# Attention and two feed-forward layers on one core: other PSUM banks for the first feed-forward, thresholds on ScalarE, mixed score tiles in four quadrants, other first and last transfers

## The chip, the core and the metric

The kernel runs on one core of a Trainium2 chip. The metric is the device time of one execution in microseconds (us), the median of the runs shown. Engines are named as in the profile: PE is the matrix engine (PEld its weight loads), DVE VectorE, ACT ScalarE, POOL GpSimd, SP the engine that issues nearly all transfers (DMAs). Each engine works through its own list of instructions in the order in which they stand there; semaphores hold an instruction until what it needs is done.

## What is computed

```python
def _attn_ref(q, k, v, tau):          # 4 batches, 8 heads, 576 tokens, head size 64
    scores = scale * np.matmul(q, k.transpose(0, 1, 3, 2))
    thresh = np.max(scores, axis=-1, keepdims=True) - tau
    scores = np.where(scores >= thresh, scores, -1000000000.0)
    scores = scores - np.max(scores, axis=-1, keepdims=True)
    attn = np.exp(scores)
    attn = attn / (np.sum(attn, axis=-1, keepdims=True) + 1e-09)
    return np.matmul(attn, v)

def _moe_ref(x, w_in, w_out, g_ln):   # 2304 tokens, 512 -> 1024 -> 512
    h = x @ w_in
    e = np.exp(h - np.max(h, axis=-1, keepdims=True))
    solu = h * (e / (np.sum(e, axis=-1, keepdims=True) + 1e-09))
    mu = np.mean(solu, axis=-1, keepdims=True)
    var = np.mean((solu - mu) ** 2, axis=-1, keepdims=True)
    return ((solu - mu) / np.sqrt(var + 1e-06) * g_ln) @ w_out

def _moe2_ref(x, w_in, w_out):        # 2304 tokens, 512 -> 2048 -> 512
    h = x @ w_in
    g = h * np.tanh(np.where(h > 20.0, h, np.log1p(np.exp(np.minimum(h, 20.0)))))
    return g @ w_out
```

Attention's output is regrouped to 2304 rows of 512, goes through the first feed-forward (`_moe_ref`) and then through the second (`_moe2_ref`).

## The kernel before

The 32 heads are worked off in 16 pairs. A pair has 576 query rows for each head: four full tiles of 128 rows for each head, and one mixed tile that holds the last 64 rows of both heads, so 9 score tiles a pair and 144 in all. For a score tile PE makes the scores in PSUM (lines 751 and 759), DVE takes the row maximum with a minus sign (line 765), ACT takes the exponential with that as its bias (line 766), POOL makes the threshold out of the same maximum, a 128x1 operation (line 768), and DVE masks the exponential by comparing score and threshold, and sums it (line 769). PE then turns the result with transposes (lines 796 to 801), ACT copies it out of PSUM (line 777), and PE multiplies it by v (line 846).

The first 8 pairs (`p < R0`) take their scores as plain float32 with the head's 64 channels split over two row halves of the array (`early`, line 751: one half makes the first 256 columns of keys, the other the last 320). A mixed tile does this twice there, once for each head, both adding into the same 128 output rows; the query columns of the other head are zeros. The last 8 pairs use split float32r products (`go`, line 759), for which ACT and POOL first make high and low parts of q and k (lines 717 to 723), with q scaled on POOL (line 721).

The first feed-forward runs on 18 tiles of 128 tokens: x times w_in (line 903), the softmax-times-h and the norm on DVE, ACT and POOL (lines 919 to 933), a transpose (line 952) and the product with w_out (line 973). Its products and transposes use two PSUM banks, `p_mo` 0 and 1, through `b_two`. Work of this stage stands between attention's score tiles, and goes on after the last of them.

The second feed-forward (line 1070) has 2016 products of 384 columns, in eight banks: six named `hoa`, which open when attention's own PSUM tiles are closed (`o_a`), and two named `hob`, which open when the first feed-forward is done (`o_c`). Its weights pass through rings of buffers `A7` and `B7`, loaded by SP; results gather in `acc` (line 1194) and leave by line 1218.

The order of all this is not written out by hand. `Plan` holds a task for each step with an engine, a duration and what it needs; `KEYS` gives each task a rank of three characters; `forward` walks through the tasks and takes for each engine the ready one with the best rank, with its own durations, rates and costs of changing PE's tile mode (`CHANGE`, by the `mode` of a task). The instructions are then written in that order, once, when the program is built. So any change of `KEYS`, of a duration or of a bank's rules gives another order on all engines.

At the start PE runs 11 products on zeros (`WARM`, line 549) while the first operands come in; ACT issues the load of tau, SP issues all others. Five small DVE operations make the scale and `nt8`, which holds minus tau, from tau (lines 552 to 556).

Of the kernel before, what the change touches and what calls it, by code (L numbers as in the profile page):

```python
# [19 lines left out]
    "io3bPeVUwaR9hdbeQVcd1hnVXPUdbHiNem8zcYDa4yca/gXgczbegzfFuaSHgQ3Y+8d3Fdl8bYnqPtfD0fHfZhWd7Rd51f+9icwYSEhLPfg2dxjb4rfZ0e+3"  # L20
    "f0Necsby5dbydYBdV1dr8aeSfWweFYfDYgpEfOjeujdbUdD9YCEdv6ibpcr4goDewob2sfaveAhb7nd6ZdjjbKlfc7Y1JdLYbvhayLa5PcwFbUpaXnfSWebq"
    "fiFaDNg7pdpGceUfQqcHYdIidYad5DcnAdeOdInaCHbjEdzTgn7cRfbYrbtceUXc7NdzLc21c5ZbuKchAfArdmxgCRc8vdLcbM+eNucswcnabINcgvZnUbJ+"
    "dwJdmWdtQboPdMcdjhdnjcRucpWccjemhbf6cAdc7YeAAcdudGbb3/eycbU8cUxbdQeJPegLa5Ad7IaWIbH1bNVciUbDIcaMbmnfxqZ2Md9kbOXW5RbYUX/1"
    "ZXPVoHYgnZflX3Dgh1cHCY8Ka2QdOsdAVY/pXSFaNrY/wbblY+aWP1ZckYhrdSpXlzVlHZ4OaoaYqeZP2ZNDX0YX4ObdYXdcZZdai/YQTYnaZMBXlpaOAbe1"
    "aaMa4QY1yYpfZqaYnCZ66WtFacBaYnbCqafKZzmYsUbCNaZLYd1YP6bDOWfiXlGbKTXwYXvnW+DXjWXS7bb2ZDCcZxZ7/WytZ7eaOEYeBadzXg8XdpXzNYRF"
    "ZuYYimXEiV3BW7IXfRZVRX+UZj+YHxXn9ZTZW7CXGPZacYyIaYHY2hZiJa5NYFKXxKXtOY1BY74ZCaY0eXOCYNWZHPXQ3X1UXjqW1qZDcXifZKSXcxUaUYYu"
    "Wt3ZcCajPXTjTdDYLEZRPa9QYEiaGvXAsZqOWaqVnMXe6YwIWhOYspYdxXjpZU+ZioYfPW3dYWbcryZLXX1MWVUb1/UjgVZJVs8ZgtWmyXS6UF5XbAZMyWW4"
    "ZNZVhOWsCW38VOcdLwWRuVaea8sXsPXM1U6NYuaWl7XWeWByV+YXhXW8IWSeUrGZO6aDYWgpX5CWx/VIsVk6V/xWi1WtPW37Uh0XBJV82b5qXoMYRiVejVN7"
    "VVzUoFWXRVuIZr+UlJXoPV2qV/hZ+KUheX4tRQvUW/UGjVoiWCHT9JaGNVrySzpXOeVsZU4yU5LYnpXCibbWZceVy4SivU1JVZhVdqWfiVAMUEeTx3Wt2TVN"
    "VVEXbeTrEXL8U//WrxUhLUsCU99WjkZSITiXWqRToEXf6UIlSphTScVeSX9iVpOTWWR5sTMtXdLYJAVaoSlDUCDUskUDOZtqXPpWCYVzrUT1WJhS+uTQ0SPn"  # L30
    "V73VbuVPiTtuYvgS8FSkLTXST9jTtLVnXVFhTzTRSLTrIUVFT8tR3qSbnVVJVGpUOkWbfTnUSeQT1TTunSCZUqmU2YU2XVjEVutTWKTZYT2NT81UpyS1ATZ1"
# [1254 lines left out]
```

## Time and profile before

| | us |
|---|---|
| median of 3 runs | 870.92 (869.85 to 874.6) |
| profiled execution | 871.98 |
| its span, first to last instruction | 870.2 |
| PE busy | 845.0 of 870.2, 97% |
| DVE busy | 738.5, 85% |
| ACT busy | 614.9, 71% |
| POOL busy | 294.1, 34% |
| TensorE clock granted | 1.00 throughout |

The busy share of an engine is an average over stages that are limited by different things. PE's busy time overlaps itself: a product's record is longer than the distance to the next one's start, so what PE really takes for a piece of work is read from one start to the next start.

### The profile page before, as it was taken

What the parts mean: (1) busy time and instruction counts of PE and PEld (TensorE: products, weight loads), DVE (VectorE), ACT (ScalarE), POOL (GpSimd) and SP (SyncE); (2) the same over time, 40 slices, a digit from 0 to 9 for tenths busy, and PEclk for the clock granted to TensorE, in tenths of its full rate; (3) what the DMA queues carried; (4) which work ended last, traced back from release to release, by engine and by line L of the source; (5) the groups of instructions that cost most, each with busy time, mean ns of one, the idle gap of its engine ahead of it and who ended that gap; (6) DMA issues with size and microseconds to landing.
All of it is one profiled execution on the core that took longest, in us unless ns stands there. A gap on an engine that the chain in (4) does not pass through costs nothing.

```text
span 870.2 us, 16492 instructions
## 1 busy us (share of the span) xinstructions
PE 845.0 (97%) x5423; PEld 736.9 (85%) x5423; DVE 738.5 (85%) x1638; ACT 614.9 (71%) x1292; POOL 294.1 (34%) x370
## 2 busy tenths in 40 slices
PE   7899999999999999999999999999999999999998
PEld 4556667878877888888789898999999999999998
DVE  6978888788788888899757897898999998968786
ACT  5898988877889878877545776856757664654551
POOL 2566665634756564532322211001121220000000
PEclk9999999999999999999999999999999999999999
DMA  7566444327745458445997689999999999888641
GB/s 238 177 210 191 141 149 127 116 77 244 207 138 151 126 158 267 132 133 151 299 391 237 193 252 325 343 306 363 305 336 302 305 298 348 279 276 275 198 136 72
DMA packets 155573, 195.22 MB, mean 224 GB/s; under 512 B 15312, under 2 KB 112608, under 8 KB 155488
## 3 DMA queue, kind: packets, MB, share of 16 engines
q1 hardware_dynamic: 155344, 194.17, 69.5%
q8 instruction: 43, 0.70, 0.3%
q14 instruction: 42, 0.34, 0.1%
q10 hardware_dynamic: 144, 0.00, 0.0%
HBM read 142.94 MB, written 51.19 MB: 223 GB/s over the span
## 4 chain that ended last, share of the span: by engine, by line
PE 83%; DVE 5%; DMA 4%; ACT 4%; issue 2%; POOL 2%; SPq 0%; POOLq 0%; ACTq 0%; DVEq 0%
PE hoa L1070 28%; PE p_mo L903 11%; PE hob L1070 9%; PE p_ta L846 9%; PE p_mo L973 9%; PE p_ta L796 6%; PE st L759 5%; PE st L751 4%; DMA B<-w2c 2%; PE p_mo L952 1%; DVE m L765 1%; DVE e L769 1%; PE p_ta L799 1%; ACT e L766 1%; DMA A<-w2c 1%
## 5 line engine op out<-in xcount | busy, mean ns | idle before, releaser
L1070 PE MATMUL hoa<-y,A 128*128 128x384 f32 x678 | 132.3, 336 | 1.8 <-ACT gf L1120 0.9
L769 DVE SCALAR_TENSOR_TENSOR e<-st,m,e 128x576 f32<-128x576 f32 x139 | 111.5, 814 | 18.0 <-POOL m L768 8.6
L765 DVE TENSOR_REDUCE m<-st 128x1 f32<-128x576 f32 x139 | 102.5, 753 | 24.6 <-PE st L751 12.4
L1070 PEld LDWEIGHTS hoa<-y,A 128*128 128x128 f32 x678 | 118.1, 188 | 3.1 <-ACT gf L1120 1.5
L766 ACT ACTIVATE e<-st,m 128x576 f32<-128x576 f32 x139 | 101.4, 741 | 23.6 <-DVE m L765 22.7
L1130 POOL TENSOR_TENSOR gf<-gf 128x384 f32<-128x384 f32 x24 | 24.4, 1017 | 232.4 <-DVE gf L1130 108.8
L1156 ACT ACTIVATE gh<-gf 128x384 fp32r<-128x384 f32 x168 | 80.4, 517 | 31.8 <-DVE gf L1130 11.5
L1070 PE MATMUL hoa<-gh,B 128*128 128x384 f32 x464 | 99.4, 335 | 0.6 <-DVE acc L1194 0.6
L1158 DVE TENSOR_TENSOR gl<-gf,gh 128x384 fp32r<-128x384 f32 x168 | 88.3, 563 | 1.5 <-PE hob L1070 1.2
L796 PE MATMUL p_ta<-ident,e 128*128 128x128 f32 x576 | 84.3, 276 | 3.7 <-ACT ex L777 1.3
L973 PE MATMUL p_mo<-LH,W2H 128*128 128x256 f32 x288 | 84.3, 293 | 1.2 <-DVE LL L958 1.2
L796 PEld LDWEIGHTS p_ta<-ident,e 128*128 128x128 f32 x576 | 65.6, 140 | 22.0 <-issue 3.6
L1070 PEld LDWEIGHTS hoa<-gh,B 128*128 128x128 f32 x464 | 82.0, 188 | 1.3 <-DVE acc L1194 1.1
L973 PE MATMUL p_mo<-LL,W2H 128*128 128x256 f32 x288 | 81.5, 283 | 0.1
L973 PE MATMUL p_mo<-LH,W2L 128*128 128x256 f32 x288 | 81.3, 282 | 0.0
L768 POOL TENSOR_SCALAR m<-m,cs 128x1 f32<-128x1 f32 x144 | 39.2, 275 | 119.8 <-DVE m L765 37.5
L612 POOL TENSOR_TENSOR ws<-cf,cl 128x512 uint32<-128x512 uint32 x32 | 41.3, 1289 | 103.5 <-DVE gl L1158 16.4
L1126 ACT ACTIVATE gf<-gf 128x384 f32<-128x384 f32 x72 | 37.2, 523 | 41.5 <-DVE gf L1123 41.2
L1194 DVE TENSOR_TENSOR acc<-acc,hoa 128x384 f32<-128x384 f32 x104 | 56.1, 550 | 8.0 <-PE hoa L1070 6.4
L903 PE MATMUL p_mo<-W1H,XH 128*128 128x512 f32 x144 | 60.8, 422 | 0.5 <-ACT ys L987 0.5
L1070 PE MATMUL hoa<-gl,B 128*128 128x384 f32 x232 | 59.2, 335 | 0.0
L973 PEld LDWEIGHTS p_mo<-LH,W2H 128*128 128x128 f32 x288 | 54.9, 191 | 3.9 <-issue 2.2
(127 smaller groups left out, 2171.0 us busy)
## 6 DMA issues: line engine op xcount, KB each, us to landing
...
```

Of the source, the lines that this page charges most:

```text
L759: TE.matmul(flat()[:, c0 + c:c0 + c + w], q.tile[:, i * 128:(i + 1) * 128], ks.tile[:, k0:k0 + w], start=(y == z == 0), stop=(y == len(hea ...
L765: t = add("DVE", dve(S), lambda: V.tensor_reduce(m.tile[:, 2:3], x(), AX.XY, ALU.max, negate=True), [t], [m], [st])
L766: a = add("ACT", act(S, True) + 0.1, lambda: SC.activation(et(), x(), ACTF.Exp, bias=m.tile[:, 2:3]), [t], [e] if h == 0 else (), [st, m, ...
L769: t = add("DVE", dve(S) + 0.06, lambda: V.scalar_tensor_tensor(et(), x(), m.tile[:, 1:2], et(), ALU.is_ge, ALU.mult, accum_out=sr.tile[:, ...
L796: TE.transpose(tp.tile[:, k * 128:(k + 1) * 128], e.tile[:, o:o + 128], ident)
L846: TE.matmul(acc.tile[h * 64:h * 64 + 64, :w], v.tile[:, k, h], r, start=(k == 0), stop=(k == KT))
L903: TE.matmul(h.tile, l.tile[:, kt], r[:, kt, j * 512:(j + 1) * 512], start=(kt == 0 and x == 0), stop=(kt == KD - 1 and x == 2))
L973: TE.matmul(y.tile[:, :PN], l[:, k, cs], r.tile[:, k], start=(k == 0 and x == 0), stop=(k == KF - 1 and x == 2))
L1070: TE.matmul(x.tile[:, :TH], l, r, start=new and n == 0, stop=stop and n == len(steps) - 1, skip_group_check=True)
L1156: a = add("ACT", act(TH), lambda h=h, x=x: SC.activation(h.tile, full(x), ACTF.Copy), [first], [h], [h, x])
L1158: out[c] = h, l, a, add(e, cost(TH), lambda h=h, l=l, x=x, eng=eng: eng.tensor_tensor(l.tile, full(x), f(h.tile), ALU.subtract), [a, *deps ...
L1194: d = add("DVE", dve(TH), lambda: V.tensor_tensor(to(), to(), fr(), ALU.add), deps + [CO.get((v, e, i, t))], use=[ac, x])
```

## The change

- `b_two.banks += ff[:6]`: the tiles of the first feed-forward may also take one of the six `hoa` banks once these are open.
- The threshold (line 768) is an ACT instruction, `Identity` with scale -1 and `nt8` as a 128x1 bias, in place of a POOL one. The scaling of q for the last 8 pairs (line 721) is an ACT copy with a 128x1 scale.
- In a mixed score tile of the first 8 pairs each head writes its own 64 output rows, from its own 64 query columns: four products on four quarters of the array, each written once, where there were four that used all 128 columns and added two by two. The task has a tile mode of its own (3).
- The first keys leave SP's queue first, and the first half of q for heads 0 and 1 is issued by ACT, behind tau; `WARM` is 9; three of the five small operations on tau are tasks of the plan.
- In the last visit each of the four result tiles leaves in two halves, each as soon as its own half is summed, with rows of 512 bytes; before in one piece with rows of 3072 bytes.
- In the plan: rates of DMAs up by 2%, `LATENCY` 1.8 for 1.5, some start times, POOL's subtraction 1.02 for 1.31, and all of `KEYS`.

```diff
@@ Plan
-    ISSUE, FIRST, LATENCY = 0.48, 0.95, 1.5
+    ISSUE, FIRST, LATENCY = 0.48, 0.95, 1.8
-    CHANGE = (0.0, 0.19, 0.135), (0.186, 0.0, 0.1), (0.1, 0.12, 0.0)
+    CHANGE = (0.0, 0.19, 0.135, 0.19), (0.186, 0.0, 0.1, 0.19), (0.1, 0.12, 0.0, 0.12), (0.186, 0.19, 0.1, 0.0)
...
-    WARM = 11
+    WARM = 9
...
-    V.tensor_scalar(t8, on, 1.0, 3.0e38, ALU.subtract, ALU.mult)
-    V.tensor_scalar(on, tau_c, 1.0, on, ALU.mult, ALU.mult)
-    V.tensor_tensor(nt8, t8, on, ALU.subtract)
+    k_c = chain("DVE", [...the same three as tasks...])
+    k_in = []
@@ operands
-            t = add("SP", dma(512 * KW, 4 * KW), lambda: D(f(ks.tile[:, :KW]), k1[n // H_, n % H_]), new=[ks])
+            first = n < 2 and not part
+            t = add(*("-", 3.6 + 0.5 * n) if first else ("SP", dma(512 * KW, 4 * KW)), lambda: D(f(ks.tile[:, :KW]), k1[n // H_, n % H_]), new=[ks], order=k_in)
...
-                q = add("SP", dma(512 * w, 4 * w), lambda c=c: D(f(qh.tile[:, c]), qq[n // H_, n % H_][:, c]), [], [qh] * (z == 0), [qh], order=OPS[n][0][1:])
+                q = add(*("-", 3.8 + 0.7 * n) if first and not z else ("SP", dma(512 * w, 4 * w)), lambda c=c, go=SC.dma_start if first and not z else D: go(f(qh.tile[:, c]), qq[n // H_, n % H_][:, c]), [], [qh] * (z == 0), [qh], order=OPS[n][0][1:] + k_in * (first and not z))
...
-        lq = add("POOL", 0.16 + SP * 0.95e-3, lambda: G.tensor_scalar(q2.tile, q2.tile, sc, 0.0, ALU.mult, ALU.add), [lq], use=[q2])
+        lq = add("ACT", act(SP), lambda: SC.activation(q2.tile, q2.tile, ACTF.Copy, scale=sc), [lq], use=[q2])
@@ s_tile
-                    TE.matmul(flat()[:, c:c + w], f(qh.tile[a, i * 128:(i + 1) * 128]), f(ks.tile[a, k:k + w]),
-                              start=(y == 0), stop=(y == len(heads) - 1))
+                    r = slice(64 * y, 64 * y + 64) if len(heads) > 1 else slice(0, 128)
+                    TE.matmul(flat()[r, c:c + w], f(qh.tile[a, i * 128 + r.start:i * 128 + r.stop]), f(ks.tile[a, k:k + w]), start=True, stop=True)
...
-        t = add("PE", pe(len(heads), KW, 4) + 0.02 if p < R0 else ...
+        t = add("PE", pe(1, KW, 4) + 0.02 if p < R0 else ...
...
-        b = add("POOL", 0.26, lambda: G.tensor_scalar(m.tile[:, 1:2], m.tile[:, 2:3], -1.0, nt8, ALU.mult, ALU.add), [t], use=[m])
+        b = add("ACT", 0.1, lambda: SC.activation(m.tile[:, 1:2], m.tile[:, 2:3], ACTF.Identity, bias=nt8, scale=-1.0), [t, k_c], use=[m])
@@ banks of the second feed-forward
+    b_two.banks += ff[:6]
@@ ff_out, results of the last visit
+                    for t in range(2):
+                        part_of = lambda x, t=t: x.rearrange("q (z t n) -> q z t n", t=2, n=128)[:, :, t]
+                        add("SP", dma(256 * TU, 512), lambda e=e, i=i, to=to, part_of=part_of: D(part_of(to()), part_of(AC[v, e, i].tile)),
+                            [CO[v, e, i, t]], use=[AC[v, e, i]])
```

ACT's list at the start of the program, before. `e` is the exponential, `m` holds maximum and threshold, `ex` and `eu` are copies out of PSUM, `cz` is weight conversion:

```order
L542 ACT_TABLE_LOAD
L551 DMA cs_130<-tau 128x1
L766 ACTIVATE e_217<-st_202,m_210 128x576
L766 ACTIVATE e_217<-st_212,m_222 128x576
L766 ACTIVATE e_242<-s3_207,m_235 128x576
L777 ACTIVATE ex_245<-p_ta0_244 128x4x128
L766 ACTIVATE e_242<-st_237,m_255 128x576
L777 ACTIVATE eu_259<-p_ta1_258 128x128
```

The same place now (line 774 is the threshold, 772 the exponential, 727 the scaling of q, 713 a load):

```order
L542 ACT_TABLE_LOAD
L551 DMA cs_130<-tau 128x1
L713 DMA Qhh_179<-qq 128x256
L713 DMA Qhh_183<-qq 128x256
L774 ACTIVATE m_212<-m_212,cs_130 128x1
L772 ACTIVATE e_220<-st_202,m_212 128x576
L772 ACTIVATE e_220<-st_209,m_217 128x576
L774 ACTIVATE m_217<-m_217,cs_130 128x1
L727 ACTIVATE Q2_190<-Q2_190,cs_130 128x640
L772 ACTIVATE e_240<-s3_214,m_234 128x576
L774 ACTIVATE m_234<-m_234,cs_130 128x1
L783 ACTIVATE ex_243<-p_ta0_242 128x4x128
```

ACT issues two loads more, and has a 128x1 instruction beside each exponential, ahead of it or behind it; 144 such and 16 of line 727 stood on POOL.

PE's list at the first mixed score tile, before. The mixed tile `st_694` takes the first four products of line 751, and a full tile follows it in the same tile mode:

```order
L796 MATMUL p_ta1_688<-ident_129,e_551 128x128 x4
L751 MATMUL st_694<-Kst_455,Qhh_467 128x256
L751 MATMUL st_694<-Kst_455,Qhh_467 128x320
L751 MATMUL st_694<-Kst_535,Qhh_513 128x256
L751 MATMUL st_694<-Kst_535,Qhh_513 128x320
L751 MATMUL st_703<-Kst_553,Qhh_542 128x256
L751 MATMUL st_703<-Kst_553,Qhh_542 128x320
```

And now, with the instructions beside it:

```order
L802 MATMUL p_ta1_686<-ident_129,e_545 128x128 x4
L805 MATMUL p_ta0_694<-ident_129,e_576 128x128
L758 MATMUL st_697<-Kst_445,Qhh_440 64x256
L758 MATMUL st_697<-Kst_445,Qhh_440 64x320
L758 MATMUL st_697<-Kst_528,Qhh_524 64x256
L758 MATMUL st_697<-Kst_528,Qhh_524 64x320
L802 MATMUL p_ta0_707<-ident_129,e_576 128x128 x4
```

The four products have 64 output rows each. Over the whole program PE goes from one tile mode to another 130 times in either order, if row halves, column halves and quarters each count as a mode.

PE's list soon after attention's last tiles, before (`p_mo` and `hoa` are banks, line 952 a transpose, line 903 the first, line 973 the second product of the first feed-forward, line 1070 the second feed-forward):

```order
L973 MATMUL p_mo1_5886<-LL_5599,W2H_133 128x256
L952 MATMUL p_mo0_5921<-ident_129,so_5626 128x128 x4
L1070 MATMUL hoa0_5928<-y7_5818,A7_5706 128x384 x6
L952 MATMUL p_mo1_5941<-ident_129,so_5626 128x128 x4
L1070 MATMUL hoa1_5950<-y7_5829,A7_5714 128x384 x6
L1070 MATMUL hoa2_5963<-y7_5692,A7_5795 128x384 x6
L903 MATMUL p_mo1_5973<-W1H_131,XH_5867 128x512
```

The same stage now (958 is the transpose, 909 the first product):

```order
L979 MATMUL p_mo0_5590<-LL_5140,W2H_133 128x256
L958 MATMUL p_mo1_5649<-ident_129,so_5187 128x128 x4
L958 MATMUL hoa0_5657<-ident_129,so_5337 128x128 x4
L958 MATMUL hoa1_5665<-ident_129,so_5187 128x128 x4
L958 MATMUL hoa2_5674<-ident_129,so_5337 128x128 x4
L909 MATMUL hoa3_5682<-W1H_131,XH_5466 128x512
L909 MATMUL hoa3_5682<-W1L_132,XH_5466 128x512
```

Two token tiles' transposes now follow each other on four banks, and the products behind them use a fifth. Counted between the 25th and the 133rd score tile, the new order has 192 products of line 903 where there were 240, 288 of line 973 where there were 336, 420 transposes of line 796 for 436, 52 of line 952 for 64: that work stands behind the 133rd tile now.

## Rows read from the trace of the kernel before

**Rows 1.** The page, busy time of PE, and the chain that ended last by engine.

```profile
PE 845.0 (97%) x5423; PEld 736.9 (85%) x5423; DVE 738.5 (85%) x1638; ACT 614.9 (71%) x1292; POOL 294.1 (34%) x370
...
PE 83%; DVE 5%; DMA 4%; ACT 4%; issue 2%; POOL 2%; SPq 0%; POOLq 0%; ACTq 0%; DVEq 0%
```

**Rows 2.** Busy time by stretch: engines in us (records), PE clock, DMA share, GB/s.

```profile
8.00:52.40 44.40, 37.48 (x260) 22.93 (x258) 39.86 (x89) 37.04 (x73) 24.02 (x45) 1.00 0.65 202
52.40:360.10 307.70, 301.78 (x2108) 232.13 (x2107) 261.90 (x573) 260.90 (x529) 178.65 (x236) 1.00 0.54 164
...
420.00:506.00 86.00, 82.48 (x525) 73.92 (x524) 63.63 (x147) 52.17 (x99) 22.83 (x18) 1.00 0.80 269
506.00:866.50 360.50, 356.59 (x2075) 353.20 (x2073) 318.08 (x701) 219.07 (x500) 43.86 (x40) 1.00 0.85 282
```

**Rows 3.** The same view for two stretches of 50 us.

```profile
250.00:300.00 50.00, 49.08 (x341) 40.55 (x340) 44.85 (x94) 44.56 (x89) 28.53 (x40) 1.00 0.48 147
...
650.00:700.00 50.00, 50.00 (x290) 50.00 (x290) 48.69 (x115) 35.38 (x81) 9.46 (x8) 1.00 0.95 298
```

**Rows 4.** PE from one start to the next: start, us, line, records.

```profile
45.49 1.89 PE L751 MATMUL st<-Kst,Qhh 64*128 64x256 f32 x12
47.31 1.95 PE L846 MATMUL p_ta<-ex,V 128*64 128x256 f32 x16
...
103.32 0.63 PE L796 MATMUL p_ta<-ident,e 128*128 128x128 f32 x4
103.87 1.24 PE L751 MATMUL st<-Kst,Qhh 64*128 64x256 f32 x8
105.04 0.33 PE L799 MATMUL p_ta<-ident,e 128*128 128x128 f32 x1
```

**Rows 5.** The chain of waits: two long pieces of the first feed-forward on PE.

```profile
409.60 7.39 PE p_mo L973 x60
...
464.66 5.55 PE p_mo L903 x24
```

**Rows 6.** Groups of ACT, 52.4 to 360.1 us: count | busy, mean | idle.

```profile
L766 ACT ACTIVATE e<-st,m 128x576 f32<-128x576 f32 x108 | 78.5, 741 | 14.2 <-DVE m L765 13.7
L777 ACT ACTIVATE ey<-p_ta 128x512 f32<-128x512 f32 x68 | 39.2, 598 | 4.5 <-PE p_ta L796 3.8
...
L920 ACT ACTIVATE em<-so,ln 128x1024 f32<-128x1024 f32 x10 | 11.5, 1152 | 0.1
L722 ACT ACTIVATE Qhh<-Q 128x640 fp32r<-128x640 f32 x15 | 11.1, 737 | 0.0
...
L928 ACT ACTIVATE ln<-ln 128x1 f32<-128x1 f32 x9 | 1.9, 209 | 0.2 <-DVE ln L927 0.2
...
L821 ACT ACTIVATE rx<-p_ta 5x128 f32<-5x128 f32 x4 | 1.0, 258 | 0.0
```

**Rows 7.** The same view of the whole run, ACT and POOL.

```profile
L1156 ACT ACTIVATE gh<-gf 128x384 fp32r<-128x384 f32 x168 | 80.4, 517 | 31.8 <-DVE gf L1130 11.5 <-PE hoa L1070 7.6 <-PE hob L1070 6.1
...
L768 POOL TENSOR_SCALAR m<-m,cs 128x1 f32<-128x1 f32 x144 | 39.2, 275 | 119.8 <-DVE m L765 37.5 <-DVE ws L662 19.2 <-DVE cz L607 12.1
```

**Rows 8.** ACT in order of time: two like instructions back to back.

```profile
853.01 0.94 ACT L1156 ACTIVATE gh<-gf 128x384 fp32r<-128x384 f32 x2 [0.31 <-DVE gf L1130]
```

**Rows 9.** Who waited for whom: us in total, times, longest; the whole run.

```profile
DVE e L769 <- POOL m L768: 8.6, 17, 1.9
```

**Rows 10.** PE's waits from 420 to 506 us, longest first.

```profile
PE p_mo L973 <- DVE LL L958: 1.2, 1, 1.2
PE p_mo L952 <- DVE LL L958: 0.7, 1, 0.7
```

**Rows 11.** The first PE work, in order of time.

```profile
1.19 4.87 PE L549 MATMUL p_ta<-warm 128*128 128x512 bf16 x11 [1.19 <-DVE warm L546]
5.99 1.19 PE L751 MATMUL st<-Kst,Qhh 64*128 64x256 f32 x4
```

**Rows 12.** The last work, in order of time.

```profile
867.05 0.33 SPq L1218 DMA_DIRECT2D out<-acc  x1
```

More of the change, by code (lines that the diff above doesn't have):

```diff
@@ L19 @@
 KEYS = (
[L20 to L31, printed above, removed]
@@ L147 @@
+    "RIYSAkQT6SC6OqpRZGOS7Qt8QRCPuIPtFP+1P+GNytTPtRyIPYBRqMP2AN14PyTRa1"
 )
@@ L553 @@
     V.tensor_scalar(sc, on, 0.125, None, ALU.mult)
-    V.tensor_scalar(t8, on, 1.0, 3.0e38, ALU.subtract, ALU.mult)
-    V.tensor_scalar(on, tau_c, 1.0, on, ALU.mult, ALU.mult)
-    V.tensor_tensor(nt8, t8, on, ALU.subtract)
-    plan = Plan({"ACT": 2.5, "DVE": 4.0, "POOL": 5.6, "SP": 0.5, "PE": 5.0}, "exp", load_table, tc)
+    plan = Plan({"ACT": 2.5, "DVE": 3.9, "POOL": 5.6, "SP": 1.5, "PE": 4.6}, "exp", load_table, tc)
     add = plan.add
@@ L567, in chain @@
         return t
+    k_c = chain("DVE", [(0.07, lambda: V.tensor_scalar(t8, on, 1.0, 3.0e38, ALU.subtract, ALU.mult)),
+                        (0.07, lambda: V.tensor_scalar(on, tau_c, 1.0, on, ALU.mult, ALU.mult)),
+                        (0.07, lambda: V.tensor_tensor(nt8, t8, on, ALU.subtract))])
+    k_in = []
     k_eye = add("SP", 0.2, lambda: D(ident, eye))
@@ L708, in operands @@
                 w = c.stop - c.start
-                q = add("SP", dma(512 * w, 4 * w), lambda c=c: D(f(qh.tile[:, c]), qq[n // H_, n % H_][:, c]), [], [qh] * (z == 0), [qh], order=OPS[n][0][1:])
+                q = add(*("-", 3.8 + 0.7 * n) if first and not z else ("SP", dma(512 * w, 4 * w)), lambda c=c, go=SC.dma_start if first and not z else D: go(f(qh.tile[:, c]), qq[n // H_, n % H_][:, c]), [], [qh] * (z == 0), [qh], order=OPS[n][0][1:] + k_in * (first and not z))
+                if first and not z:
+                    k_in[:] = [q]
                 eng, e, cost = (V, "DVE", dve2(w)) if n < 2 and not part else (G, "POOL", 0.16 + w * 0.95e-3)
@@ L760, in go @@
                                   start=(y == z == 0), stop=(y == len(heads) - 1 and z == 1))
-        t = add("PE", pe(len(heads), KW, 4) + 0.02 if p < R0 else pe(4 * len(heads), S / 2) + 0.07, early if p < R0 else go,
-                [t for o in ops for t in o[0][:2 if p == 0 and i < 2 else None]], [st], slots, mode=int(p < R0))
+        t = add("PE", pe(1, KW, 4) + 0.02 if p < R0 else pe(4 * len(heads), S / 2) + 0.07, early if p < R0 else go,
+                [t for o in ops for t in o[0][:2 if p == 0 and i < 2 else None]], [st], slots, mode=(p < R0) * (1 if i < KT else 3))
         EXS.append([t])
```

253 lines of the change are left out of this document (134 added, 119 removed).

## The prediction

> **What bounds the kernel now.** I read the page first: the busy times of the engines and the chain that ended last [rows 1]. PE is busy 845.0 of 870.2 us and holds 83% of that chain, so the time is PE's list of work plus what PE loses. Then the busy time by stretch, to see who stands next to PE in each [rows 2, 3]. In the second feed-forward (506 to 866.5 us) nobody is near: the best 50 us have PE at 50.00 with DVE at 48.69 and ACT at 35.38. In attention, from the exponential of the 25th score tile (52.4 us) to that of the 133rd (360.1 us), PE is busy 301.78 of 307.7, and DVE and ACT carry nearly the same load, 261.90 and 260.90, POOL 178.65. There ACT can become the bound, and the change moves all of POOL's thresholds to ACT: this stretch decides. Last, PE in order of time, the groups of ACT, and the waits [rows 4 to 12].
>
> **Busy time is not need.** Busy time counts overlapped records once, so it says too little of what an engine has to spare. Two like exponentials of line 1156 took 0.94 us back to back, where one has a mean of 0.517 [rows 7, 8]: 2 x 0.517 - 0.94 = 0.09, say 0.10, is overlap. What ACT needs for an instruction is its duration less 0.10. The groups of ACT in the stretch, the 108 exponentials at 741 ns first and 4 copies at 258 ns last, 529 records in all, come to 300.6 us by count times mean [rows 6]; less 529 x 0.10 this is 247.7 us, 0.81 of the stretch. For PE I take the distance from one start to the next.
>
> **The stretch from 52.4 to 360.1 us: what PE loses of work.** By the order of the new kernel 48 products of line 903, 48 of line 973, 16 transposes of line 796 and 12 of line 952 now stand behind the 133rd tile. 24 of line 903 took 5.55 us (0.231 each) and 60 of line 973 took 7.39 (0.123) [rows 5]; four transposes took 103.87 - 103.32 = 0.55 (0.138 each) [rows 4]. So 11.1 + 5.9 + 28 x 0.138 = 20.9 us leave the stretch, and are paid again behind it.
>
> A mixed tile: 12 records of line 751, one mixed tile and one full tile, took 47.31 - 45.49 = 1.82 us; 8 records, two full tiles, took 105.04 - 103.87 = 1.17 [rows 4]. A full tile is 0.585, the mixed one 1.235. If four quarters work side by side as two halves do, the 8 new records take half: 0.62 less. Bounds: 0 (quarters take turns) and 0.65 (it costs a full tile). I take 0.62, since row halves with columns of 64 and of 128 already run at this pace. Seven of the eight tiles lie in the stretch: 4.3 us. The eighth lies ahead, where PE waits anyway, and counts nothing.
>
> PE changes its tile mode as often as before, 130 times, so that costs nothing either way. The Trainium skill, TensorEngine Tiling (Array Packing), Key Properties, says that tiles of 64 x 64 run as four at once and that a change of mode needs a drain; no row of before shows quarters.
>
> PE's need in the stretch, its present losses kept, is then 307.7 - 20.9 - 4.3 = 282.5 us.
>
> **What ACT gets there.** 109 thresholds and 15 scalings of q come, and some copies and exponentials of the first feed-forward leave with its moved work. A 128x1 instruction without a pointer operand has 209 ns (line 928), so needs 0.11. The exponential, with a pointer bias, takes 741 for 576 columns, where a copy takes 598 for 512 [rows 6]. By the slope from 517 at 384 columns [rows 7] to 737 at 640 [rows 6], 0.86 ns a column, 64 columns are 55 ns; the other 88 are the pointer's. A threshold should so need 0.11 + 0.09, less a little since the two estimates share rounding: 0.18. Bounds: 0.11, the pointer free, and 0.28, no overlap at all. A scaling of q is line 722's 737 plus 0.09 less 0.10: 0.73. Together 109 x 0.18 + 15 x 0.73 = 30.6. What leaves: 2 of 1152 (line 920), 2 like them (line 926), and ten copies of around 598 or less, 8.7 in all. ACT's need: 247.7 + 30.6 - 8.7 = 269.6 us.
>
> The Trainium skill, ScalarE: Activation LUTs, What ACT_TABLE_LOAD costs, gives an ACTIVATE 186 ns plus 0.833 a column, 93 more for each pointer operand, and 93 of overlap, so by that page a threshold is an estimate of 187 ns, and all 144 are 26.9 us of ACT. By that price the 109 are 20.4 us, in place of my 19.6. It speaks against the change: ACT was given work that POOL did beside it.
>
> So the two engines nearly meet: PE 282.5, ACT 269.6. What share of a stretch can ACT spend so? Need to busy time was 247.7 to 260.9, 0.95, here. In its best 50 us ACT was busy 44.56 [rows 3], by that ratio a need of 42.3 or 0.85, with PE the bound. DVE was busy 48.69 of 50 beside PE at 50.00 [rows 3], by that ratio 0.92, and held PE up nowhere. So 0.85 and 1 are the bounds; I take 0.95, a little over what DVE shows to be possible: 269.6 / 0.95 = 283.8, and with two engines so close some of either's idle time is not hidden: **284.5 us**, 23.2 less than now. With 20.9 paid behind, the stretch brings **-2.3 us**.
>
> POOL's threshold ended 8.6 us of DVE's waits before line 769, 17 times [rows 9]. These go, but the threshold now stands in ACT's list, beside exponentials, copies and PE's next operands, and whoever is queued behind it on ACT waits 0.18. I count the gain at nothing, as ACT is the nearer limit; its bounds are 0 and -6.6 (8.6 less the waits at the very start).
>
> **The start.** Eleven products on zeros took 4.87 us and the first scores began at 5.99 [rows 11]. Two fewer: 2 x 4.87 / 11 = 0.9 earlier at most, if keys and q have landed by then; the first keys stand first on SP's queue now and q leaves through ACT, whose two issues stand ahead of its first exponential, when ACT has nothing to do. Against it, up to 52.4 us ACT is busy 37.04 of 44.4 and gets 24 thresholds, 4.3 us [rows 2]; PE, at 37.48, waits here for DVE and ACT. Bounds -0.9 and +4.3, nearer to the first since ACT has 7 us idle: **-0.5**.
>
> **The first feed-forward behind attention.** From 420 to 506 us PE is busy 82.48 of 86 [rows 2]; its longest waits are for copies out of the two banks (1.2, 0.7) [rows 10]. With up to eight banks transposes and products of several token tiles follow each other, and these waits have cover. But the 20.9 us come here too, with their DVE and ACT work, and DVE has 22 us to spare in 86. Bounds -3.5 (all idle) and +1.5 (the second feed-forward's opening products find fewer `hoa` banks); I take **-2.5**.
>
> **The second feed-forward and the end.** PE is busy 356.59 of 360.5 [rows 2] with the same 2016 products: 0, bounds of 2 on either side for weights that land at other times. The last issue starts at 867.05 and the span ends at 870.2 [rows 12]: 3.15 us for one piece. With two halves, the first leaves while the second is summed; what comes after the last sum is half the data but rows of 512 bytes. Bounds -1.0 and +0.4 (one issue of 0.33 more in the queue): **-0.5**.
>
> POOL's subtraction, rates and latency are numbers of the plan and act through the order alone.
>
> **Sum.** -2.3 - 0.5 - 2.5 - 0.5 = -5.8. The profiled execution took 871.98 (span 870.2, 1.8 around it), 1.06 over the median 870.92; from the profiled one it gives 866.2, from the median **865.1 us**.
>
> **Rivals.** (1) ACT becomes the bound. If it cannot spend more than 0.89 in the stretch, this takes 269.6 / 0.89 = 302.9, 18.4 more than I forecast: 883.5. For it: the best 50 us, 0.85; ACT takes things in order, and a copy for PE then stands behind a threshold that waits for DVE's maximum. Against: ACT's exponentials waited 14.2 us for DVE in the stretch [rows 6], so it had no need to be fuller. It decides from a share of 0.915 downward (294.7 us; 875.3 in all). (2) PE binds alone: thresholds overlap fully, and DVE's 8.6 us of waiting for POOL go as well. Then the stretch is 282.5 less some 4 of PE's losses, 278.5: 859.1. For it: PE's share of the chain; against: ACT's load. (3) Quarters take turns, and the mixed tiles save nothing: 4.3 more on PE's side, 869.4. For it: no row shows quarters. (4) The second feed-forward's weights come later, since the DMAs were given other times: bound 3.3 or more, 868 to 871. For it: the DMA share there is 0.85 [rows 2], 0.95 at its best [rows 3]; against: the same bytes.
>
> **Chances.** Forecast 0.40 (861 to 868.5), ACT bound 0.17 (875 to 890), PE alone 0.25 (855 to 861), quarters 0.08, weights 0.10. A measurement here tells apart about 0.5%: faster is under 866.6, slower over 875.3. Faster: all of PE alone and three quarters of the forecast, 0.55; slower: most of the ACT case, 0.15; within: 0.30. The range leaves out a tenth at either end: 857.0 to 877.0.
>
> **What would show it.** Thresholds at about 0.28 us a record (0.37 if the pointer costs double), exponentials waiting less for DVE and more for ACT's own list. The 25th to 133rd exponential some 284 us apart; over 295 ACT is the bound, and ACT's idle time there is nearly gone, under 280 PE was alone. Mixed tiles of 8 records with 0.6 us to the next start; 1.2 would mean turns. First scores at about 5.2 us. From 420 us to the first feed-forward's end no wait of PE over 0.5 us for line 958's successors. The end 2.6 us after the last issue. I am wrong if the stretch alone gives back more than 2.3 us net, or if PE's losses behind 506 us, now 3.9, have grown.

## The result, and the profile after

| | before | after |
|---|---|---|
| median of 20 runs, us | 872.29 (869.85 to 874.6) | 877.36 (871.35 to 881.74) |
| profiled execution, its span | 871.98, 870.2 | 877.32, 875.5 |
| ratio to before | | 1.0058, 95% interval 1.0042 to 1.0073 |

The change made the kernel 5 us slower; 5.8 us less were forecast (865.1, from a median of 3 runs), and the time lies just above the range. The page after, as [rows 1]:

```profile
PE 847.8 (97%) x5421; PEld 734.0 (84%) x5421; DVE 739.8 (84%) x1638; ACT 648.0 (74%) x1452; POOL 244.3 (28%) x210
...
PE 71%; ACT 10%; DMA 7%; DVE 5%; issue 2%; POOL 1%; SPq 0%; ACTq 0%; POOLq 0%; DVEq 0%
```

ACT holds 10% of the chain that ended last where it held 4%, PE 71% where it held 83%. By stretch, with the columns of [rows 2] (first row: from the 25th to the 133rd score tile by PE's first product of each):

```profile
57.40:348.90 291.50, 284.71 (x1991) 212.75 (x1992) 248.20 (x542) 270.98 (x622) 133.67 (x108) 0.99 0.50 152
354.50:506.00 151.50, 150.87 (x1013) 134.70 (x1013) 122.55 (x285) 107.08 (x216) 45.58 (x35) 1.00 0.74 240
510.00:871.50 361.50, 355.21 (x2066) 350.69 (x2064) 316.15 (x696) 216.43 (x494) 42.05 (x37) 1.00 0.83 276
```

ACT is now busy 270.98 of 291.5 us in attention (0.93, before 0.85). In the first feed-forward PE has 0.63 us of idle time in 151.5 us; in the second 6.3 of 361.5, where [rows 2] has 3.9 of 360.5. The groups of ACT and the waits of VectorE's mask that answer to [rows 6] and [rows 9], whole run; in each block the first line is of the kernel before, the others are of the changed one:

```profile
L766 ACT ACTIVATE e<-st,m 128x576 f32<-128x576 f32 x139 | 101.4, 741 | 23.6 <-DVE m L765 22.7 <-PE p_ta L799 0.4
L774 ACT ACTIVATE m<-m,cs 128x1 f32<-128x1 f32 x144 | 41.4, 295 | 9.4 <-DVE m L771 8.8
L772 ACT ACTIVATE e<-st,m 128x576 f32<-128x576 f32 x139 | 101.2, 740 | 3.5 <-DVE m L771 3.1
```

```profile
DVE e L769 <- ACT e L766: 6.8, 19, 1.0
...
DVE e L775 <- ACT e L772: 18.5, 34, 1.7
...
DVE e L775 <- ACT m L774: 5.9, 18, 0.9
```

ACT waits only 3.5 us ahead of its exponentials (before 23.6): when it comes to one, the maximum is nearly always there already. VectorE's mask, which waited 8.6 us for POOL's threshold and 6.8 for the exponential, now waits 5.9 for the threshold and 18.5 for the exponential. ACT is not busy throughout: 20.5 us of the stretch are idle.

PE in order of time: the start, and a mixed tile.

```profile
1.19 3.44 PE L549 MATMUL p_ta<-warm 128*128 128x512 bf16 x9 [1.19 <-DVE warm L546]
5.09 0.81 PE L758 MATMUL st<-Kst,Qhh 64*128 64x256 f32 x4 [0.47 <-DVE Qhh L717]
...
8.84 0.77 PE L758 MATMUL st<-Kst,Qhh 64*128 64x320 f32 x4 [1.33 <-DVE e L775]
9.55 0.33 PE L802 MATMUL p_ta<-ident,e 128*128 128x128 f32 x1
...
47.69 0.77 PE L758 MATMUL st<-Kst,Qhh 64*64 64x256 f32 x8
48.39 1.09 PE L802 MATMUL p_ta<-ident,e 128*128 128x128 f32 x8
```

A mixed tile's 8 records take 0.70 us to the next start (48.39 - 47.69), as the 4 records of a full tile do that stands alone (9.55 - 8.84 = 0.71); 1.235 were read before. The four quarters run side by side.

TensorE's granted clock, which was 1.00 throughout, falls to 1.2 of 2.4 GHz three times (columns: length, PE busy and its records, clock, DMA share, GB/s):

```profile
7.00:10.50 3.50, 2.17 (x16) 1.00 1.03 263
10.50:14.50 4.00, 4.00 (x17) 0.57 0.96 337
35.00:38.00 3.00, 0.94 (x8) 1.00 0.74 257
38.00:41.50 3.50, 3.50 (x16) 0.51 0.15 48
55.50:58.50 3.00, 1.17 (x9) 1.00 0.24 89
58.50:62.00 3.50, 3.50 (x16) 0.51 0.83 266
```

Each fall comes behind a gap of PE, 1.33 us at 7.5, 2.11 at 35, 1.83 at 55.6, in which it waited for VectorE's mask.

### The profile page after: what moved, and what is told of

Its sections match the earlier page's. It is cut to its first block, busy times and chain, and to the rows that moved or that the text cites. A ratio compares the mean times of both kernels' runs of the same rounds, so it can differ in the third digit from the quotient of the medians.

```text
span 875.5 us, 16405 instructions
## 1 busy us (share of the span) xinstructions
PE 847.8 (97%) x5421; PEld 734.0 (84%) x5421; DVE 739.8 (84%) x1638; ACT 648.0 (74%) x1452; POOL 244.3 (28%) x210
## 4 chain that ended last, share of the span: by engine, by line
PE 71%; ACT 10%; DMA 7%; DVE 5%; issue 2%; POOL 1%; SPq 0%; ACTq 0%; POOLq 0%; DVEq 0%
PE hoa L1077 27%; PE hob L1077 8%; PE p_mo L979 7%; PE p_ta L852 6%; PE p_mo L909 6%; PE p_ta L802 5%; PE st L765 4%; ACT e L772 3%; PE st L758 3%; PE hoa L979 2%; DMA y<-yc 2%; PE hoa L909 2%; DVE e L775 1%; DMA A<-w2c 1%; ACT m L774 1%
## 5 line engine op out<-in xcount | busy, mean ns | idle before, releaser
L775 DVE SCALAR_TENSOR_TENSOR e<-st,m,e 128x576 f32<-128x576 f32 x139 | 112.2, 814 | 25.8 <-ACT e L772 18.5
L1077 PE MATMUL hoa<-gh,B 128*128 128x384 f32 x568 | 121.6, 335 | 0.7 <-DVE acc L1201 0.7
L1077 PE MATMUL hoa<-y,A 128*128 128x384 f32 x588 | 116.0, 337 | 1.1 <-ACT gf L1127 0.6
L1077 PEld LDWEIGHTS hoa<-y,A 128*128 128x128 f32 x588 | 102.2, 188 | 3.0 <-ACT gf L1127 1.8
L1077 PEld LDWEIGHTS hoa<-gh,B 128*128 128x128 f32 x568 | 100.2, 188 | 1.4 <-DVE acc L1201 1.0
L1077 PE MATMUL hoa<-gl,B 128*128 128x384 f32 x284 | 72.1, 334 | 0.0
L979 PE MATMUL p_mo<-LH,W2H 128*128 128x256 f32 x224 | 65.8, 294 | 0.2 <-ACT so L916 0.2
L979 PE MATMUL p_mo<-LL,W2H 128*128 128x256 f32 x224 | 63.3, 283 | 0.0
L979 PE MATMUL p_mo<-LH,W2L 128*128 128x256 f32 x224 | 63.2, 282 | 0.0
L758 PE MATMUL st<-Kst,Qhh 64*128 64x256 f32 (+3 forms) x300 | 50.0, 450 | 4.5 <-DVE e L775 3.3
L783 ACT ACTIVATE ey<-p_ta 128x512 f32<-128x512 f32 x80 | 47.4, 604 | 6.0 <-PE p_ta L802 5.4
```

Source lines behind the costliest of these rows:

```text
L758: TE.matmul(flat()[r, c:c + w], f(qh.tile[a, i * 128 + r.start:i * 128 + r.stop]), f(ks.tile[a, k:k + w]), start=True, stop=True)
L775: t = add("DVE", dve(S) + 0.06, lambda: V.scalar_tensor_tensor(et(), x(), m.tile[:, 1:2], et(), ALU.is_ge, ALU.mult, accum_out=sr.tile[:, ...
L979: TE.matmul(y.tile[:, :PN], l[:, k, cs], r.tile[:, k], start=(k == 0 and x == 0), stop=(k == KF - 1 and x == 2))
L1077: TE.matmul(x.tile[:, :TH], l, r, start=new and n == 0, stop=stop and n == len(steps) - 1, skip_group_check=True)
```

## The experiments

In all of them but one (f3) the plan is computed as it stands, and only what an instruction is, or on which engine, is changed where it is written, or products on zeros are added: the order of everything else is word for word kept. Times are medians; "before" ran beside them at 871.6 to 872.8.

### Who makes the thresholds

e1, the changed kernel with POOL; e3, the kernel before with ACT:

```diff
 e1   b = add("ACT", 0.1, ...)            # place in the plan kept
-     SC.activation(m[1:2], m[2:3], Identity, bias=nt8, scale=-1.0)
+     G.tensor_scalar(m[1:2], m[2:3], -1.0, nt8, mult, add)
 e3   the reverse, in the kernel before
```

> The changed kernel with one thing undone: the 144 thresholds are POOL instructions again, at the same places of the program; the lists of PE, DVE and SP are word for word those of the changed kernel, ACT's list lacks only the thresholds. Theory 1 (thresholds in ACT's list delay exponentials and copies, PE stands still for 2.1 us at 35 and 1.8 us at 56, and the granted clock then falls): these two gaps shrink below 1.3 us, the clock's mean rises from 0.993 to 0.997 or more, and the time falls by 4 us or more, to 873 or less. Theory 2 (the new order and its ring of score banks make the gaps, whoever makes the thresholds): gaps and clock stay, the time stays within 2 us of 877.4. Theory 3 (POOL is late for an order made for ACT): over 880.

> The kernel before with one thing changed: the 144 thresholds are ACT instructions, at the places in the program where POOL's stood; all other lists are word for word the same. Theory 1 (a threshold costs ACT 0.18 to 0.2 us and delays what stands behind it, 26 to 29 us of ACT in all, with ACT at four fifths of its time in attention): slower by 2 to 8 us, 874.5 to 880. Theory 2 (DVE's 8.6 us of waiting for POOL end and ACT has room): faster by 1 to 4 us, 868 to 871.

e1: 891.9 (1.0203, 1.0177 to 1.0229). e3: 883.3 (1.012, 1.0098 to 1.0142), clock 1.00. In e1 theory 3 holds, in e3 theory 1, above its range. The waits of both:

```profile
DVE e L775 <- POOL m L774: 29.4, 50, 1.5
```

```profile
DVE e L769 <- ACT m L768: 25.0, 47, 1.6
```

An order made for one engine's thresholds makes the other engine late: VectorE waits 25 to 29 us. So neither tells what a threshold costs in an order made for it. f1 and f2 do, by leaving them out; that part of the softmax is then not computed:

```diff
-     b: threshold;   mask: x >= m[1:2]
+     b: nothing;     mask: x >= m[2:3]
```

> The changed kernel with the 144 threshold instructions left out (the mask compares with the maximum in their place, so this part of the softmax is not computed); the other instructions stand in the same order on every engine. It shows what the thresholds cost in ACT's list all told. Theory 1 (they do: some 0.19 us each, 27 us of ACT, and DVE's waits for them make PE's gaps at 35 and 56 us): at least 5 us faster than 877.4, clock 0.997 or more. Theory 2 (the order and the score banks bind PE, not the thresholds): within 2 us of 877.4, the gaps and the falls of the clock stay.

> The kernel before with the 144 threshold instructions left out in the same way (that part of the softmax is not computed), order of all else kept. It shows what POOL's thresholds cost there. Theory 1 (POOL's thresholds hold up DVE and through it PE, 8.6 us of waits): 3 to 6 us faster than 872.5. Theory 2 (those waits have cover): less than 1.5 us faster. If theory 2 holds, there was nothing to gain by taking the thresholds from POOL.

f1: 865.7 (0.9925, 0.9905 to 0.9945). f2: 871.6 (0.9999, 0.9985 to 1.0012). By the times theory 1 in the first and theory 2 in the second: on POOL, in the order of before, the thresholds cost **nothing**, within 1.3 us; on ACT, in the new order, **11.6 us**. All the rest of the change is worth 865.7 - 871.6 = -5.9.

Of theory 1 of f1 only the time came true. PE's gaps stay without thresholds, and so do falls of the clock (its mean is 0.994 in the profile; 0.997 was expected):

```profile
35.53 1.11 PE L802 MATMUL p_ta<-ident,e 128*128 128x128 f32 x4 [2.01 <-DVE e L775]
```

The kernel before has no gap of PE longer than 1.1 us between 10 and 120 us, so it is the new order that makes them, not the thresholds.

k4 takes the cost apart: ACT makes each threshold, nobody reads it, and the mask compares with the maximum.

```diff
-     SC.activation(m[1:2], ...);   mask: x >= m[1:2]
+     SC.activation(m[8:9], ...);   mask: x >= m[2:3]
```

> The changed kernel in which ACT makes the 144 thresholds at their places, but into a column that nobody reads; the mask compares with the maximum (that part of the softmax is not computed). ACT's time is as in the changed kernel, and VectorE's mask does not wait for a threshold. Theory 1 (ACT's time in its list costs the 11.6 us): within 2 us of 877.4. Theory 2 (VectorE's wait for the threshold in each tile's chain costs them): near 865.7, below 869. Between: both.

873.5 (1.0023, 1.0008 to 1.0037): between the theories. 873.5 - 865.7 = 7.7 us come with the thresholds in ACT's list alone, 877.4 - 873.5 = 3.9 when the mask reads them too (8.5 and 3.1 by the ratios to the kernel before). What VectorE's masks wait for exponentials, in f1 and in k4:

```profile
DVE e L775 <- ACT e L772: 10.4, 21, 1.7
...
DVE e L775 <- ACT e L772: 19.5, 38, 1.7
```

So thresholds that nobody reads make the exponentials late for the mask by 9 us in all. That the 3.9 are the mask's wait for the threshold is not shown: in the two profiles the changed kernel and k4 are 0.7 us apart at the 133rd tile (348.85 and 348.20), and the rest of their difference lies behind it, where 11 thresholds are left.

g1 puts them on VectorE, which is less busy than ACT in attention (248.2 and 271.0 us above):

```diff
-     V.tensor_reduce(m[2:3], ...)                 SC.activation(m[1:2], ...)
+     V.tensor_reduce(m[2:3], ...); V.tensor_scalar(m[1:2], m[2:3], -1.0, nt8, mult, add)
```

> The changed kernel with the 144 thresholds on VectorE, each right behind its row maximum; all else in the same order. Without any thresholds the changed kernel took 865.7 us. Theory 1 (what costs is that ACT, full and in order, makes them; DVE has room, and its mask then waits for no other engine's threshold): some 0.09 us each, 13 us of DVE mostly hidden: 866 to 870. Theory 2 (DVE is as full as ACT, so the cost only moves): 874 or more.

879.1 (1.0079, 1.0054 to 1.0104): theory 2. A threshold there has 0.214 us and stands in each tile's own chain of maximum and mask:

```profile
L771 DVE TENSOR_SCALAR m<-m,cs 128x1 f32<-128x1 f32 x144 | 30.9, 214 | 5.1
```

m1 shares them out, 51 on ACT and 93 on POOL, and m2 adds the products on zeros told below:

```diff
+     ON_ACT = the 51 tiles whose threshold came later than exponential and VectorE in e1
-     SC.activation(m[1:2], ...)
+     SC.activation(m[1:2], ...) if in ON_ACT else G.tensor_scalar(m[1:2], ...)
```

> The changed kernel with its thresholds shared out: 51 stay on ACT, those whose threshold came later than exponential and VectorE in the run with all of them on POOL; the other 93 are POOL's. Order of all else kept. With all on ACT 877.4, with all on POOL 891.9, with none 865.7. Theory 1 (ACT's time and the wait cost in proportion to the thresholds that ACT makes, and POOL's cost nothing where they are in time): 865.7 + 51/144 of 11.6 = 870 us, within 2. Theory 2 (POOL is late with others now, since its list is taken in order too): 876 or more.

> The same with the 20 products on zeros in four of PE's gaps. Theory 1 (the falls of the clock cost 1 to 2 us, as with the thresholds all on ACT): 1 to 2 us faster than without them, 868 to 869. Theory 2 (no gap is long enough now): the same time.

m1: 871.2 (0.999, 0.997 to 1.001), theory 1: 865.7 + 51/144 x 11.6 = 869.8 within its 2 us. 6 of the 11.6 us come back. m2: 871.1 (0.9994, 0.9978 to 1.001), no faster than m1: theory 2 by the time, but not for its reason, since the mean clock rose from 0.996 to 0.998.

### Scaling of q, quadrants, banks

```diff
 g3 -  SC.activation(q2, q2, Copy, scale=sc)
 g3 +  G.tensor_scalar(q2, q2, sc, 0.0, mult, add)
 e4 +  the quadrants, in the kernel before
 f4 -  the quadrants, in the changed kernel
 f3 +  b_two.banks += ff[:6]     # in the kernel before; the plan gives another order
```

> The changed kernel with the 16 scalings of q on POOL again, order of all else kept. They take ACT 0.73 us each, 11.7 us in all. Theory 1 (every us of ACT counts in attention, as the thresholds do: 11.6 us for some 27 of ACT): 4 to 5 us faster, 872 to 873. Theory 2 (they stand where ACT has time, or POOL is late with them): within 1.5 us of 877.4.

877.0 (1.0047, 1.0029 to 1.0065): theory 2. Taking 11.7 us from ACT gains nothing that shows. VectorE's masks wait for exponential and threshold as before it (17.0 and 5.5 us, 18.5 and 5.9 in the changed kernel), and POOL is not late with the scalings: ACT waits 0.9 us for them.

> The kernel before with one thing changed: the first 8 mixed score tiles in four quadrants, order of all other instructions kept. In the changed kernel a mixed tile took about what a full one takes, so about 0.6 us less each. Theory 1 (PE binds): 8 times 0.6 come out in full, 4 to 5 us faster, 867.3 to 868.3. Theory 2 (DVE or ACT end last where the mixed tiles stand): less than 2 us faster. Theory 3 (PE waits instead of working, and the clock falls): no faster, clock below 1.00.

> The changed kernel with the first 8 mixed tiles made as before (two heads added into the same 128 rows), order of all else kept. Before with quadrants gained 2.1 us (0.9978), not 4.6. Theory 1 (in the changed kernel PE is not the bound where they stand, so they hide too): slower by 2.5 us or less. Theory 2 (PE is the bound there): slower by 4 to 5. Theory 3 (shorter mixed tiles make PE's gaps longer and the clock falls oftener): not slower, with a higher clock.

e4: 870.7 (0.9978, 0.9962 to 0.9993), 2.1 us faster than the 872.8 beside it, at the upper edge of theory 2. f4: 879.9 (1.0083, 1.0056 to 1.0111), 2.5 slower than the changed kernel, theory 1; the intervals of the two overlap, so this difference is not clear of noise.

How much work the quarters save depends on what stands beside them. A mixed and a full tile one behind the other, in the kernel before and in e4, and a mixed tile alone in f4:

```profile
107.52 1.89 PE L751 MATMUL st<-Kst,Qhh 64*128 64x256 f32 x12 [1.01 <-DVE e L769]
109.34 0.87 PE L846 MATMUL p_ta<-ex,V 128*64 128x256 f32 x6
...
106.89 1.51 PE L752 MATMUL st<-Kst,Qhh 64*64 64x256 f32 x12 [1.01 <-DVE e L769]
108.33 1.51 PE L846 MATMUL p_ta<-ex,V 128*64 128x256 f32 x12
...
49.05 1.35 PE L757 MATMUL st<-Kst,Qhh 64*128 64x256 f32 x8
50.33 0.87 PE L802 MATMUL p_ta<-ident,e 128*128 128x128 f32 x6
```

In the order of before the pair takes 1.44 where it took 1.82, and 0.28 to 0.38 are saved at seven of the eight places, 2.3 us together: what e4 gains is about all of it, so theory 2's reason does not hold. In the new order the mixed tile takes 1.28 without quarters and 0.70 with them; over the eight 4.4 us are saved, and 2.5 show.

> The kernel before with one line added: the first feed-forward may also use the six banks that attention frees. The plan puts out another order from there on (first and second feed-forward), the part up to attention's end is word for word the same. Theory 1 (PE's waits from 420 to 506 us go): 2.5 us faster, 869 to 871. Theory 2 (it is worth more, as the changed kernel's smaller losses behind 426 us suggest): 4 to 6 us faster. Theory 3 (what the first feed-forward gains the second loses, since its first weights and products come at other times): within 1 us.

927.5 (1.063, 1.0606 to 1.0654), beyond all three theories. Two of PE's waits:

```profile
PE hob L1070 <- ACT B L1097: 11.0, 1, 11.0
PE hoa L1070 <- DMA A<-w2c: 5.8, 5, 2.4
```

The ranks were not made for these banks; the new order has PE wait 11 us for one weight tile. The worth of the banks alone can't be had by this edit; it stays open by itself.

### The start and the clock

```diff
 e2 -  WARM = 9
 e2 +  WARM = 11
 g2 +  TE.matmul(bank, zeros, zeros 128x512) x4 at 7.5 us, x6 at 35, x6 at 55.6, x4 at 85
 g4 +  the same in g1
```

> The changed kernel with 11 products on zeros at the start where it has 9; nothing else. Theory 1 (the fall of the clock at 10.7 us comes from the shorter run of products ahead of the first gap): the clock is 1.00 from 8 to 16 us, the mean rises by 0.002, and of the 0.8 us that the first scores start later most is given back: 875.5 to 877. Theory 2 (the gap of 1.3 us alone does it): the fall stays, and the time is up to 0.8 us longer, 877.4 to 878.2.

877.3 (1.0054, 1.0033 to 1.0075). The time lies between the two theories, and its interval covers both. The first fall is gone as theory 1 says: behind a gap of 1.79 us at 7.95 the clock stays,

```profile
7.00:10.50 3.50, 1.71 (x13) 1.00 0.85 274
10.50:14.50 4.00, 3.32 (x22) 1.00 0.94 335
```

PE is busy 3.32 of the 4 us there and waits for the rest, as the changed kernel's PE worked through all 4 at a lower clock.

But that the two products more kept the clock up is not shown. With 9 products, as in the changed kernel, the first fall is missing too in the profiles of e1, f1, g3 and m1: the clock is 1.00 from 8 to 35 us behind gaps of 1.37 to 1.79 us at 7. In those of f4, g1 and k4 it falls once in that time. Whether it fell changed from one execution to the next.

> The changed kernel with 20 products on zeros more, of 512 columns, put into four of PE's gaps: 4 at 7.5 us, 6 at 35, 6 at 55.6 and 4 at 85 us (the last ones add zeros to an open sum). Nothing else is moved; they take 0.2 us each and lie within gaps of 1.3 to 2.1 us. Theory 1 (the falls of the granted clock behind these gaps, 3.4 us each at half speed, cost time of their own): clock 0.998 or more, 4 to 5 us faster, 872 to 873.5. Theory 2 (the gaps cost what they cost, and PE's slow stretches lie where it would wait anyway): the clock rises, the time stays within 1.5 us of 877.4.

> The changed kernel with both: the thresholds on VectorE and the 20 products on zeros in PE's gaps. Theory 1 (the two costs are separate and add): as the one with the thresholds on VectorE less 3 to 5 us, 862 to 866, the clock 0.998 or more, below both kernels. Theory 2 (with shorter gaps the products on zeros are in the way, or the clock holds anyway): no faster than with the thresholds on VectorE alone.

In g2 the clock stays up behind the gap at 35:

```profile
35.00:38.00 3.00, 2.13 (x11) 1.00 0.77 242
38.00:41.50 3.50, 3.48 (x28) 1.00 0.30 108
```

g2: 876.0 (1.0036, 1.0018 to 1.0054), clock 0.998: 1.4 us, theory 2. g4: 876.7 (1.0049, 1.0031 to 1.0066), clock 0.999, 2.4 less than g1 and between its theories. Over the 20 runs of the changed kernel the mean clock goes from 0.990 (881.7) to 1.000 (871.35), which looks like 10 us of clock; kept up by hand it was worth 1.4 (g2), 2.4 (g4) and nothing (m2). The intervals overlap each time, so 0 to 2.4 us is a size, not a proof. Low clock and long time may have a common cause, the gaps; no run shows this by itself.

### A mask without a threshold

Another way to be rid of the thresholds is to compare the exponential with exp(-tau), one number for all rows; k2 does it in the kernel before with the quadrants, k3 adds the products on zeros to k1.

```diff
-     mask: (x >= m[1:2]) * e        # x in PSUM, e in SBUF
+     mask: (e >= exp(-tau)) * e     # both in SBUF
```

> The changed kernel without threshold instructions, the mask made another way: VectorE compares the exponential itself with exp(-tau), one number for all rows, and no longer reads the scores a second time, so a score bank comes free after the exponential and not after the mask. Order of all else kept. Without thresholds but with the bank held until the mask it took 865.7 us. Theory 1 (each tile's chain of maximum, exponential and mask on few score banks is what binds attention): at least 3 us below 865.7. Theory 2 (the engines' own time binds, not the banks): 864 to 867.

> The kernel before with the quadrants (870.7 alone) and the mask made from the exponential as in the run above, no thresholds on any engine, order of all else kept. Without thresholds the kernel before was no faster. Theory 1 (the chain on few score banks binds there too): 866 or less. Theory 2 (in that order PE's list and the engines' time bind): 869 to 871.

> The changed kernel with the mask made from the exponential and the 20 products on zeros in four of PE's gaps. With the thresholds on ACT these products raised the clock from 0.993 to 0.998 and brought 1.4 us. Theory 1 (they keep the clock up and PE is nearer to being the bound now): 1 to 4 us faster than without them. Theory 2 (gaps are shorter now, the products stand in the way): no faster.

k1: 888.8 (1.0201, 1.0172 to 1.023); k2: 895.8 (1.0262, 1.0244 to 1.028); k3: 890.6 (1.0215, 1.0198 to 1.0233). k3 is no faster than k1, its theory 2; of k1 and k2 all theories missed, for a reason none had (the last three lines are VectorE and POOL in order of time):

```profile
L775 DVE SCALAR_TENSOR_TENSOR e<-e,cs 128x576 f32<-128x576 f32 x144 | 152.0, 1073 | 9.6 <-ACT e L772 8.3
...
L775 DVE SCALAR_TENSOR_TENSOR e<-e,cs x144: 758/817/2101, 7.7 to 414.6; 128x576 f32<-128x576 f32 x144
...
59.87 0.81 DVE L775 SCALAR_TENSOR_TENSOR e<-e,cs 128x576 f32<-128x576 f32 x1
60.09 1.72 POOL L628 TENSOR_TENSOR W1L<-cf,W1H 128x512 fp32r<-128x512 f32 x1 [0.89 <-ACT W1H L627]
60.60 1.83 DVE L775 SCALAR_TENSOR_TENSOR e<-e,cs 128x576 f32<-128x576 f32 x1
```

The mean mask takes 1.073 us where it took 0.814 with one operand in PSUM, 144 x 0.26 = 37 us more of VectorE. But the median (0.817) has not moved. 92 of the 144 take 0.82 us or less, among them all 53 that ran while POOL rested; the other 52 take 0.87 to 2.10, and during each of them POOL is at work for more than a third of the time. POOL's instruction is held up as well: 1.72 us here, 1.27 on average for line 628 in the changed kernel. There, with one operand in PSUM, 71 masks met POOL so, and none took more than 0.82. So two operands in SBUF cost nothing by themselves; what costs is that VectorE and POOL then hold each other up. The plan keeps VectorE's instructions that are marked `port` apart from POOL's; this mask, which read PSUM, has no such mark, and the edit gave it none. What freeing the score bank early is worth was not learnt.

No version that computes everything beat both kernels clearly but e4, the kernel before with the quadrants alone, by 0.2%.

## Why the prediction was wrong, point by point

**What bounds the kernel** was read right in the main: ACT and PE nearly meet in attention, and that stretch holds 6.8 of the 11.1 us between forecast and profile (table below). The forecast's own sign for it, the distance of two exponentials (284 expected, over 295 ACT is the bound), leaves it open: the 25th and the 133rd, which it names, lie 354.5 - 59.0 = 295.5 apart, those that it had read 343.4 - 55.5 = 287.9. A slip in naming the stretch: 52.4 to 360.1 us are the exponentials of the 23rd and the 131st tile, while the work moved was counted from the 25th to the 133rd. By PE's first products those two start at 54.5 and 362.4 us, 307.8 apart where 307.7 was used, so the sum stands. After, they start at 57.4 and 348.9. Line 1156, from which the overlap of 0.10 was read, is a copy and not an exponential; the figure held all the same.

| part of the program, us | forecast | profiled execution |
|---|---|---|
| to the 25th score tile | -0.5 | 57.4 - 54.5 = +2.9 |
| 25th to 133rd | -23.2 | 291.4 - 307.8 = -16.4 |
| behind, with the 20.9 moved there | 20.9 - 2.5 - 0.5 = +17.9 | 526.7 - 507.8 = +18.8 |
| sum | -5.8 | +5.3 |

The stretch net of the work moved is 20.9 - 16.4 = 4.5 us longer than before, where 2.3 shorter was forecast. The third row is of one profile each: in eight other runs whose list of PE is the same there (e1, e2, f1, g1, g3, k1, k4, m1), that part took 522.6 to 526.7 us.

**PE's work.** A mixed tile's 0.62 was near: 0.43 to 0.58 against f4, in the same order. Rival 3, quarters in turn, fell. That a mixed tile between tiles of the other mode saves only 0.28 to 0.38 (e4) was not foreseen. The Trainium skill, TensorEngine Tiling (Array Packing), Key Properties, says that different tiles can execute in parallel; this trace agrees, with 0.70 us for four quarters' 8 records.

**A threshold's price** was right: two starts in ACT's list lie 0.19 apart (27.95 and 28.14 below), 0.18 was forecast. The estimate of 187 ns from the Trainium skill, ScalarE: Activation LUTs, What ACT_TABLE_LOAD costs, agrees with this. ACT's need was right too: duration less 0.10, summed over the stretch's records, gives 265.9 us, forecast 269.6.

```profile
27.95 0.28 ACT L774 ACTIVATE m<-m,cs 128x1 f32<-128x1 f32 x1
28.14 0.73 ACT L772 ACTIVATE e<-st,m 128x576 f32<-128x576 f32 x1
```

**The share that failed.** The step that failed is the one from ACT's need to time: "I take 0.95, a little over what DVE shows to be possible". ACT reached 265.9 / 291.4 = 0.913, and the stretch took 6.9 us more than the forecast 284.5. Without thresholds (f1) it takes 285.6, so 5.8 of them go with the thresholds. VectorE's 0.92 was shown in the second feed-forward, and by ACT's ratio of need to busy time; in attention ACT and VectorE pass each tile to and fro. Rival 1, ACT becomes the bound, is nearest; its own point of decision was a share of 0.915, for 875.3 us, and it got a chance of 0.17.

The runs show more than a share that was too high: no share gives the time. ACT spends 0.929 in k4 (268.8 of 289.2 us), and only 0.875 in g3 (254.6 of 291.0), which is no shorter than the changed kernel. ACT's work counts by where it stands: scalings of q, 11.7 us, cost nothing, and thresholds beside the exponentials, some 27 us of ACT, cost 7.7 though nobody read them, as VectorE's masks then wait for later exponentials. That a late mask then holds up a score bank, and so PE, is argued and not shown; k1, meant to test it, did not.

The 11.6 us are medians' worth. In the profiles 5.8 lie in the stretch and 2.1 ahead of it; the remaining 4.0 lie behind the 133rd tile, and k4, with thresholds on ACT too, does not have these, so it is open whether the thresholds cost them.

**POOL's 8.6 us of waits** "go, I count the gain at nothing": the price was right, f2 shows that they cost nothing. So by the forecast's own terms moving the thresholds could only lose, and it said that the price speaks against the change. But 8.6 us of waits for POOL became 5.9 for the threshold and 11.7 more for the exponential (18.5 for 6.8).

**The start**: the first scores at 5.09 as forecast, 0.9 earlier, but the 25th tile is 2.9 us late. The -0.5 was taken near the wrong bound; ACT's 24 thresholds there were worth 2.1 (55.3 in f1), the other 0.8 belongs to the rest of the change, whose order has PE wait 2.1 us at 35, and 2.0 in f1 without thresholds.

**The first feed-forward**: right. PE's idle time from the 133rd exponential to 506 us fell from 3.5 (141.5 - 137.98) to 0.63, -2.9 against -2.5.

**The second**: 0 with bounds of 2, and in this profile +2.4, waits for loads of y and A (1.6 and 1.5 us). In other runs with the same order there PE's idle time is 3.8 to 4.0 (f1, g1, g3), 5.2 (e2) and 5.7 (m1); with the order of before it is 2.6 (f2) to 4.1 (e4). So it changes from run to run, and the new order may cost 1 to 2 us here: rival 4 is neither shown nor excluded at that size.

**The end**: nothing gained. From the start of the last sum to the end 875.5 - 871.8 = 3.7 us, before 870.2 - 866.5 = 3.7; -0.5 was forecast.

**What f1 and f2 leave open**: the -5.9 of all but the thresholds is, as an estimate, 2 to 2.5 of quadrants (e4, f4) and some 3 of the first feed-forward in its order and banks (the 2.9 above); order and banks can't be parted by an edit that keeps the order.
